# Bucketed attention with a SwiGLU behind it: batch 1's second pair turned and hashed in other slots, one scaling on ScalarE, one pair's loads on ScalarE's queue

## The chip, the core and the metric

The kernel runs on one core of a Trainium2 chip. The core has TensorE (PE, matrix products; PEld is its weight load), VectorE (DVE), ScalarE (ACT), GpSimd (POOL) and SyncE (SP, which here only issues DMAs), each with its own instruction stream that it works through in order. The metric is the device time of one execution in microseconds (us). A comparison of two kernels on this chip tells them apart from about 2%, here 6.8 us.

## The reference

Four batches, eight heads, 768 tokens, head width 64. Each token's query and key is hashed by six sign bits of a projection; a query sees only the keys of its own bucket. The attention output goes through an RMS norm and a SwiGLU with width 1536.

```python
q_bits = (np.einsum('bhsd,dk->bhsk', q, proj) > 0).astype(np.int64)
k_bits = (np.einsum('bhsd,dk->bhsk', k, proj) > 0).astype(np.int64)
q_bucket = np.sum(q_bits * powers, axis=-1)
k_bucket = np.sum(k_bits * powers, axis=-1)
mask = q_bucket[:, :, :, None] == k_bucket[:, :, None, :]
scores = np.where(mask, scale * q @ k.T, -1e9)
attn = softmax(scores)
x = (attn @ v).transpose(0, 2, 1, 3).reshape(B * S, H * D)
xn = x / sqrt(mean(x * x) + 1e-6) * rms_g
g = xn @ w_gate
out = (g * sigmoid(g)) * (xn @ w_val) @ w_out
```

## The kernel before, in words

The mask is folded into the score product: each head's operand (tile QK) has 64 rows of q or k and 12 rows of scaled sign bits, so that a score whose buckets differ is so low that its exponential vanishes. A **pair** (b, hp) is two heads of one batch. For a pair, these steps make QK:

- the raw k and q are loaded (lines 111 and 121, tiles kL and qL);
- they are turned. Batch 0 and the first two pairs of batch 1 are turned by TensorE (`keep_pair`: three transposes at line 169 into a PSUM bank, then a copy by DVE at line 177 into kT or qT); the others by DVE itself from 32-wide blocks (`turn_dve`, line 193, four steps for k and four for q);
- they are cast to 16 bits into QK (lines 183 and 185 in halves by ACT and POOL, or line 201 whole by POOL);
- they are hashed (`hash_pair` or `hash_lone`: eight products at line 209 into d_ps, the signs by DVE at line 216, and eight small SP DMAs, line 267 or 284, that put the bit rows into QK).

A **window** w is half of a batch's queries (w = 2b or 2b + 1). The work runs in 192 **slots**, one for each (window, head, third of the keys): in a slot PE computes the scores of the next slot (line 343, two PSUM buffers), ACT takes their exponential (line 353) and later PE multiplies with v (line 365). The first 48 slots are windows 0 and 1 (batch 0); slots 48 to 71 are window 2. When a pair of heads of a window is done, `attn_out` divides (lines 380 to 401) and `sumsq` sums the squares (line 405). After a window, `norm` takes the sums (DVE, line 412) and the root (POOL, lines 414 and 418), `scale_x` scales three chunks of 128 rows (line 423), `turn_x` turns them (PE line 430, DVE line 431). The SwiGLU of window w starts in slot 24w + 48: gate (line 445, tanh by ACT at line 447), value (line 455, DVE lines 457 and 458), projection (line 469).

The order is written by hand: `at(s, f, ...)` puts a step into slot s, and inside a slot steps go by rank, then by order of entry. Steps with rank under 3 come ahead of the slot's exponential, the others behind it. Since each engine is in order, a step that waits holds up all that was put behind it on its engine. SP's stream holds the k, q and v loads and the bit rows; POOL's holds the casts, half of `attn_out`, the sums of v and the loads of the SwiGLU weights (lines 520 and 526, software DMAs); ACT's holds no DMA between the first microsecond and the last.

PSUM banks for all but scores and attention outputs come from one ring of three ("g"). Raw tiles come from a ring of ten.

Of the kernel before, what the change touches and what calls it, by code (L numbers as in the profile page):

```python
# [43 lines left out]
def kernel(  # L44
# [12 lines left out]
    nc = tc.nc  # L57
# [38 lines left out]
    raw = {}  # L96

    def raw_tile(b, hp, which):
        shape = [128, 24, 32] if which != "v" and (b, hp) not in BY_PE else [128, 2, 6, D]
        raw[b, hp, which] = lpool.tile(shape, FP32, name=which + "L", tag="L")  # L100
        return raw[b, hp, which]
# [10 lines left out]
        else:  # L112
            eng.dma_start(out=t[:, heads[0]], in_=src[:, heads[0]])

    def load_blocks(eng, b, hp, which):
        lt = raw_tile(b, hp, which)
        for hh in range(2):
            src = {"q": q, "k": k}[which][b, 2 * hp + hh].rearrange("(t k) d -> t k d", k=24)
            for dc in range(2):
                p0 = 64 * hh + 32 * dc  # L120
                eng.dma_start(out=lt[p0 : p0 + 32], in_=src[:, :, 32 * dc : 32 * dc + 32])

# [206 lines left out]
    x, ssp, xn, xnT, ht = {}, {}, {}, {}, {}  # L331
# [76 lines left out]
    rstds = {}  # L408
# [11 lines left out]
    def scale_x(w, c):  # L420
        if w not in xn:
            xn[w] = npool.tile([128, 3, DMODEL], FP16, name="xn")
        nc.vector.tensor_scalar_mul(xn[w][:, c, :], x[w][:, c, :], rstds[w][:, c : c + 1])  # L423

    def turn_x(w, c):
        if w not in xnT:
# [146 lines left out]
    def at(s, f, *a, rank=3):  # L573
        plan[s].append((rank, len(plan[s]), lambda: f(*a)))
# [36 lines left out]
    for i, (t, src) in enumerate(((wg, moe_w_gate), (wv, moe_w_val))):  # L611
        at(2 + 4 * i, load_w, t, src, 0, 768)
        at(12 + 9 * i, load_w, t, src, 768, 1536)
        at(33 + 6 * i, load_wo, 6 * i, 6 * i + 6)

    for hp, loads, turns, sv in ((0, (9, 11, 15), (24, 26, 28, 30), 42),
                                 (1, (13, 17, 28), (33, 35, 37, 39), 45)):
        for which, s in zip("kqv", loads):  # L620
            at(s, load_rows, nc.sync, 1, hp, which)
        for i, s in enumerate(turns):
            at(s, keep_pair, 1, hp, i)
            at(s + 1, casts, 1, hp, i)
        at(turns[3] + 2, hash_pair, 1, hp)
        at(sv, v_prep, 1, hp)
        at(sv + 2, v_sum, 1, hp)

    def in_row(loads, s, hash_slot=None):
        return loads, range(s, s + 8), (s + 4, s + 8, s + 9), hash_slot

    work = {
        (1, 2): ((21, 23, 30), (36, 37, 40, 40, 48, 49, 50, 51), (42, 52, 46), 53),
        (1, 3): in_row((42, 44, 47), 52, 61),
        (2, 0): in_row((51, 56, 59), 61), (2, 1): in_row((64, 67, 70), 71, 80),
        (2, 2): in_row((73, 76, 79), 81), (2, 3): in_row((82, 85, 88), 91, 100),
        (3, 0): in_row((94, 98, 102), 106), (3, 1): in_row((104, 108, 112), 116, 125),
# [1 line left out]
    }  # L641
    for (b, hp), (loads, turns, cast_slots, sh) in work.items():
        for which, s in zip("kqv", loads):
            at(s, load_rows if which == "v" else load_blocks, nc.sync, b, hp, which)
        for i, s in enumerate(turns):
            at(s, turn_dve, b, hp, "kq"[i // 4], i % 4, rank=5)
        for which, s in zip("kq", cast_slots):
            at(s, cast_pool, b, hp, which)
        if sh:
            if b == 1:  # L650
                at(sh, hash_lone, b, hp)
            else:
                at(sh, hash_pairs, b, (hp - 1, hp))
        at(cast_slots[2], v_prep, b, hp)
        at(cast_slots[2], v_sum, b, hp)
        if hp % 2:
            at(66 if b == 1 else 48 * b + (17 if hp == 3 else -4), v_mean, b, hp - 1, 4)
# [17 lines left out]
    for w in range(8):  # L675
        for h in range(H):
            end = LAST[w, h] + 3
            at(end - 1, av, w, h, 0, 9)
            at(end, av, w, h, 9, 18)
            if h % 2:  # L680
                at(end, o_step, w, h // 2, rank=4.5)
                if (w, h) != (0, 7):
                    at(end + 6, s_step, w, h // 2, rank=5)
        at(end + (1 if w == 0 else 9), norm, w, rank=5)
        for c in range(3):
            at(end + (3 if w == 0 else 14 + c), scale_x, w, c, rank=5)
            at(end + (7 + c if w == 0 else 17 + 2 * c), turn_x, w, c, rank=1)
        s0 = 24 * w + 48
        seen = set()
        for ft in range(NF):  # L690
            for f, s in ((g_step, s0 + 16 * ft // NF), (v_step, s0 + (32 * ft + 16) // (2 * NF))):
                at(s, f, w, ft, rank=4 if s in seen else 2)
                seen.add(s)
        for i in range(9 if w < 7 else 6):
            c, j = divmod(i, 3)
            at(s0 + 16 + i, project, w, c, 4 * j, 4 * j + 4, rank=1 if i == 8 else 3)
# [61 lines left out]
```

## Time and profile before

| what | value |
|---|---|
| runs | 340.42 us median of three, 337.58 to 343.3 |
| the profiled execution: its time, its span | 339.3 us, 337.5 us |
| granted TensorE clock | 0.999 |
| busy share: PE, DVE, ACT, POOL | 97%, 70%, 62%, 46% |
| exponentials on ACT (line 353) | 192 of 808 ns |
| DMA issues by SP of 32-wide k and q blocks | 80 |
| DMA issues by ACT | 2, both at the ends |

The span is the time from the first to the last instruction of the core; what lies around it is 1.8 us. A row of a timeline gives the start, the length, the engine, the line and operation, the tiles and the count; a bracket at its end gives how long the engine stood idle before it and for whom. A name with q (SPq, POOLq) is a sequencer: it issues or waits and counts as idle. In a row of waits stand the total, the number of times and the longest.

### The profile page before, as it was taken

Reading aid. Unit: us, or ns where it says so; the run is one execution under the profiler, and the core shown is the slowest. Engines: PE = TensorE matmul, PEld = TensorE weight load, DVE = VectorE, ACT = ScalarE, POOL = GpSimd, SP = SyncE. Lnnn points to the kernel's source line nnn. Section 1 sums busy time; section 2 is a strip of 40 time slices with the busy share of each in tenths; the row PEclk is TensorE's granted clock in tenths of the full one; section 3 lists DMA queues with packets and bytes.
Section 4 is the critical chain, followed back from the end, with each engine's and each line's share of the span. In section 5 each row is a group of like instructions: output and inputs, shape, how many; then the busy total and the mean of one; then the engine's idle time right before and its main releaser. Section 6 shows DMA issues by size and latency. Waiting matters only on the chain.

```text
span 337.5 us, 7796 instructions
## 1 busy us (share of the span) xinstructions
PE 326.8 (97%) x2993; PEld 201.0 (60%) x2993; DVE 236.4 (70%) x526; ACT 210.0 (62%) x328; POOL 155.3 (46%) x230
## 2 busy tenths in 40 slices
PE   8999989889999999999999999999999999999995
PEld 7566656455566565566555666566556665655653
DVE  4769798688758896668768897557546663883860
ACT  3789987656666575757666676567667675332321
POOL 4878789836465576245736475613111311110000
PEclk9999999999999999999999999999999999999999
DMA  7999999464376064508243261100010001001002
GB/s 238 330 223 260 169 169 187 75 124 100 79 186 118 15 111 119 104 20 168 69 105 84 44 116 64 35 16 0 33 62 2 3 0 64 33 0 64 32 0 93
DMA packets 80244, 31.36 MB, mean 93 GB/s; under 512 B 65240, under 2 KB 77264, under 8 KB 80208
## 3 DMA queue, kind: packets, MB, share of 16 engines
q1 hardware_dynamic: 76272, 26.09, 31.7%
q0 software_dynamic: 3712, 4.72, 8.8%
q8 instruction: 23, 0.38, 0.5%
q14 instruction: 13, 0.11, 0.1%
q10 hardware_dynamic: 224, 0.07, 0.1%
HBM read 28.32 MB, written 6.29 MB: 103 GB/s over the span
## 4 chain that ended last, share of the span: by engine, by line
PE 85%; DVE 6%; SPq 3%; DMA 2%; ACT 2%; issue 1%; DVEq 0%; ACTq 0%
PE y_ps L469 18%; PE v_ps L455 17%; PE s_ps L343 15%; PE g_ps L445 12%; PE o_ps L365 9%; PE s_ps L445 5%; PE d_ps L209 4%; SPq L267 2%; PE t_ps L169 1%; PE x_ps L430 1%; PE z_ps L336 1%; DMA kL<-in_k_dram 1%; DVE otmp L380 1%; DVE xn L423 1%; ACT psb L353 1%
## 5 line engine op out<-in xcount | busy, mean ns | idle before, releaser
L353 ACT ACTIVATE psb<-s_ps 128x768 f16<-128x768 f32 x192 | 150.8, 808 | 28.1 <-PE s_ps L343 26.9
L343 PE MATMUL s_ps<-QK 76*128 76x384 f16 x384 | 93.5, 325 | 1.3 <-ACT psb L353 0.5
L455 PE MATMUL v_ps<-xnT,wv 128*128 128x384 f16 x384 | 78.1, 326 | 0.1
L469 PE MATMUL y_ps<-wo,ht 128*128 128x512 f16 x276 | 69.2, 379 | 0.3 <-ACT ysb L476 0.3
L389 POOL TENSOR_TENSOR x<-otmp,rcp 128x384 f32<-128x384 f32 x31 | 25.7, 830 | 93.0 <-DVE rcp L385 92.7
L365 PEld LDWEIGHTS <-psb 128*128 128x128 f16 x1152 | 51.6, 97 | 25.5 <-issue 7.5
L447 ACT ACTIVATE t<-g_ps 128x384 f32<-128x384 f32 x72 | 35.3, 490 | 43.6 <-PE g_ps L445 43.4
L458 DVE SCALAR_TENSOR_TENSOR ht<-a,v_ps 128x384 f16<-128x384 f32 x96 | 53.2, 554 | 10.7 <-PE v_ps L455 1.5
L457 DVE SCALAR_TENSOR_TENSOR a<-t,g_ps 128x384 f32<-128x384 f32 x72 | 39.5, 548 | 28.5 <-ACT t L447 28.3
L445 PE MATMUL g_ps<-xnT,wg 128*128 128x384 f16 x288 | 58.6, 325 | 0.7 <-DVE a L457 0.5
L365 PE MATMUL o_ps<-vl,psb 128*128 128x65 f16 x1152 | 56.8, 194 | 0.6 <-DVE otmp L380 0.5
L455 PEld LDWEIGHTS <-wv 128*128 128x128 f16 x384 | 36.4, 97 | 23.9 <-issue 0.5
L445 PEld LDWEIGHTS <-wg 128*128 128x128 f16 x384 | 36.0, 97 | 24.4 <-issue 1.1
L343 PEld LDWEIGHTS <-QK 76*128 76x128 f16 x384 | 31.6, 98 | 16.1 <-issue 3.7
L469 PEld LDWEIGHTS <-ht 128*128 128x128 f16 x276 | 25.9, 97 | 24.0 <-issue 0.6
L476 ACT COPY ysb<-y_ps 128x512 f32<-128x512 f32 x23 | 13.5, 585 | 25.5 <-PE y_ps L469 22.8
L431 DVE TENSOR_TENSOR xnT<-x_ps,gcol 128x512 f16<-128x512 f16 x24 | 16.3, 685 | 15.1 <-PE x_ps L430 15.1
L401 POOL TENSOR_TENSOR sq<-x 128x384 f32<-128x384 f32 x31 | 25.6, 826 | 2.4
L380 DVE TENSOR_TENSOR otmp<-o_ps,cvb 128x390 f32<-128x390 f32 x32 | 17.8, 558 | 8.8 <-PE o_ps L365 8.7
L447 ACT ACTIVATE t<-s_ps 128x384 f32<-128x384 f32 x24 | 11.8, 491 | 18.4 <-PE s_ps L445 17.6
L201 POOL CAST QK<-kT 64x768 f16<-64x768 f32 x20 | 16.8, 838 | 12.4 <-DVE kT L193 6.5
L193 DVE STREAM_TRANSPOSE kT<-kL 128x192 f32<-128x192 f32 x40 | 19.8, 517 | 2.7 <-DMA kL<-in_k_dram 2.7
(80 smaller groups left out, 325.7 us busy)
## 6 DMA issues: line engine op xcount, KB each, us to landing
vL<-in_v_dram SPq DMA_DIRECT2D x16, 384.0 KB
out_dram<-ysb SPq DMA_DIRECT2D x23, 256.0 KB
kL<-in_k_dram SPq DMA_DIRECT2D x40, 96.0 KB
qL<-in_q_dram SPq DMA_DIRECT2D x40, 96.0 KB
kL<-in_k_dram SPq DMA_DIRECT2D x5, 384.0 KB
qL<-in_q_dram SPq DMA_DIRECT2D x5, 384.0 KB
wg<-in_moe_w_gate_dram POOLq DMA_DIRECT2D x2, 768.0 KB, 7.2
wv<-in_moe_w_val_dram POOLq DMA_DIRECT2D x2, 768.0 KB, 8.5
```

Of the source, the lines that this page charges most:

```text
L343: nc.tensor.matmul(ps[:, j, 0:HALF], k_cols(w // 2, h, 2 * p + j), q_cols(w, h), start=True, stop=True,)
L353: nc.scalar.activation(psb[w, h][:, p], sps.pop(g)[:, :, 0:HALF], AF.Exp, scale=ESCALE,)
L365: nc.tensor.matmul(o[:, c, hh, 0:65], psb[w, h][:, jt // 2, jt % 2, 128 * c : 128 * c + 128], vls[b % 2][:, h, v_chunk(b, h, jt), 0:65], s ...
L380: nc.vector.tensor_add(tmp[:, :, :, 0:65], o[:, :, :, 0:65], cvb[b % 2][:, 2 * hp : 2 * hp + 2, 0:65].unsqueeze(1).to_broadcast([128, 3, 2 ...
L389: eng.tensor_mul(xd.rearrange("p c (h d) -> p c h d", h=2), tmp[:, :, :, 0:64], r.to_broadcast([128, 3, 2, 64]),)
L401: nc.gpsimd.tensor_mul(sq, xd, xd)
L445: nc.tensor.matmul(g, wg[:, kt, fs], xnT[w][:, kt], start=(kt == 0), stop=(kt == 3))
L447: nc.scalar.activation(t, g, AF.Tanh, scale=0.5)
L455: nc.tensor.matmul(vv, wv[:, kt, fs], xnT[w][:, kt], start=(kt == 0), stop=(kt == 3))
L457: nc.vector.scalar_tensor_tensor(out=a, in0=t, scalar=1.0, in1=g, op0=ALU.add, op1=ALU.mult)
L458: nc.vector.scalar_tensor_tensor(out=ht[w][:, ft], in0=a, scalar=0.5, in1=vv, op0=ALU.mult, op1=ALU.mult)
L469: nc.tensor.matmul(y, ht[w][:, ft, c * 128 : (c + 1) * 128], wo[:, ft, :], start=(ft == 0), stop=(ft == NF - 1),)
```

## The change

Slots move for batch 1's first three pairs; two steps change their engine.

- Pair (1, 1): the four `keep_pair` go from slots 33, 35, 37, 39 to 31, 32, 33, 34, each with its casts one slot later; its hash goes from 41 to 40. The norm of window 0 stays in slot 39.
- Pair (1, 0): hash stays in slot 32; `v_prep` goes from 42 to 36. Pair (1, 1): `v_prep` goes from 45 to 48 and `v_sum` from 47 to 50.
- Pair (1, 2): q's load goes from slot 23 to 33, v's from 30 to 38; the third DVE turn of k goes from 40 to 37; k's cast goes from 42 to 46; `v_prep` and `v_sum` go from 46 to 52.
- Pair (1, 3): the k and q blocks are issued by ACT instead of SP, one block a slot: k in slots 46 to 49, q in 50 to 53 (before: all four of k in slot 42, all four of q in 44), last in their slot.
- The two halves of w_out are issued by POOL in slots 38 and 49 (before 33 and 39).
- The sum of squares of window 0's third pair comes one slot sooner (37).
- Chunk 1 of window 0 is scaled by ACT (`nc.scalar.mul`, slot 41), the other chunks still by DVE.

```diff
-    def load_blocks(eng, b, hp, which):
-        lt = raw_tile(b, hp, which)
-        for hh in range(2):
+    def load_blocks(eng, b, hp, which, parts=range(4)):
+        lt = raw.get((b, hp, which)) or raw_tile(b, hp, which)
+        for i in parts:
+            hh, dc = divmod(i, 2)
             src = {"q": q, "k": k}[which][b, 2 * hp + hh].rearrange("(t k) d -> t k d", k=24)
-            for dc in range(2):
-                p0 = 64 * hh + 32 * dc
-                eng.dma_start(out=lt[p0 : p0 + 32], in_=src[:, :, 32 * dc : 32 * dc + 32])
+            eng.dma_start(out=lt[32 * i : 32 * i + 32], in_=src[:, :, 32 * dc : 32 * dc + 32])
...
-        nc.vector.tensor_scalar_mul(xn[w][:, c, :], x[w][:, c, :], rstds[w][:, c : c + 1])
+        if (w, c) == (0, 1):
+            nc.scalar.mul(xn[w][:, c, :], x[w][:, c, :], rstds[w][:, c : c + 1])
+        else:
+            nc.vector.tensor_scalar_mul(
+                xn[w][:, c, :], x[w][:, c, :], rstds[w][:, c : c + 1]
+            )
...
-        at(33 + 6 * i, load_wo, 6 * i, 6 * i + 6)
+        at(38 + 11 * i, load_wo, 6 * i, 6 * i + 6)
...
-    for hp, loads, turns, sv in ((0, (9, 11, 15), (24, 26, 28, 30), 42),
-                                 (1, (13, 17, 28), (33, 35, 37, 39), 45)):
+    for hp, loads, turns, sv, ss, sh in (
+        (0, (9, 11, 15), (24, 26, 28, 30), 36, 44, 32),
+        (1, (13, 17, 28), (31, 32, 33, 34), 48, 50, 40),
+    ):
...
-        at(turns[3] + 2, hash_pair, 1, hp)
+        at(sh, hash_pair, 1, hp)
         at(sv, v_prep, 1, hp)
-        at(sv + 2, v_sum, 1, hp)
+        at(ss, v_sum, 1, hp)
...
-        (1, 2): ((21, 23, 30), (36, 37, 40, 40, 48, 49, 50, 51), (42, 52, 46), 53),
-        (1, 3): in_row((42, 44, 47), 52, 61),
+        (1, 2): ((21, 33, 38), (36, 37, 37, 40, 48, 49, 50, 51), (46, 52, 52), 53),
+        (1, 3): in_row((46, 50, 47), 52, 61),
...
-            at(s, load_rows if which == "v" else load_blocks, nc.sync, b, hp, which)
+            if which == "v":
+                at(s, load_rows, nc.sync, b, hp, which)
+            elif (b, hp) == (1, 3):
+                for i in range(4):
+                    at(s + i, load_blocks, nc.scalar, b, hp, which, [i], rank=6)
+            else:
+                at(s, load_blocks, nc.sync, b, hp, which)
...
-                    at(end + 6, s_step, w, h // 2, rank=5)
+                    at(end + (5 if (w, h) == (0, 5) else 6), s_step, w, h // 2, rank=5)
```

## The prediction

> **What bounds the kernel now.** First the busy shares of the page, then a table of stretches (columns: stretch, length, busy us with instructions of PE, PEld, DVE, ACT and POOL, then clock, DMA share, GB/s).
>
> ```profile
> PE 326.8 (97%) x2993; PEld 201.0 (60%) x2993; DVE 236.4 (70%) x526; ACT 210.0 (62%) x328; POOL 155.3 (46%) x230
> ```
>
> ```profile
> 30.00:41.00 11.00, 10.46 (x139) 6.77 (x133) 8.32 (x18) 10.45 (x16) 9.66 (x16) 1.00 1.03 223
> 41.00:54.00 13.00, 11.60 (x140) 7.65 (x137) 12.27 (x29) 10.88 (x17) 10.34 (x16) 1.00 1.03 187
> 54.00:66.00 12.00, 11.70 (x119) 7.16 (x119) 8.67 (x19) 8.07 (x13) 11.29 (x17) 1.00 0.59 98
> 66.00:70.50 4.50, 2.34 (x15) 1.18 (x13) 3.12 (x8) 1.36 (x3) 0.88 (x2) 1.00 0.94 184
> 70.50:100.00 29.50, 29.43 (x275) 17.60 (x274) 21.81 (x51) 18.94 (x30) 17.92 (x24) 1.00 0.53 112
> ```
>
> PE is the bound: 97% over the span, and from 70.5 us on it hardly pauses (29.43 of 29.50). Every moved step lies before that point. From 30 to 41 ACT is full (10.45 of 11.00), from 41 to 54 DVE is (12.27 of 13.00), from 66 to 70.5 nobody is. PE's pauses are 1.40 us in 41 to 54, 0.30 in 54 to 66 and 2.16 in 66 to 70.5: 3.86 us, 1.1% of the time, is about all that can be won back.
>
> The view of waits from 30 to 75 us names what ended the pauses (total, times, longest):
>
> ```profile
> DVE kT L193 <- DMA kL<-in_k_dram: 2.7, 1, 2.7
> ...
> PE m_ps L324 <- DVE bits L216: 1.6, 1, 1.6
> ...
> PE d_ps L209 <- DVE qT L177: 0.9, 1, 0.9
> ```
>
> The timeline gives their places. Round the hash of pair (1, 1) in slot 41, first DVE alone, then all engines, then the scalings and the first gate:
>
> ```profile
> 48.77 0.54 DVE L177 COPY qT<-t_ps 128x384 f32<-128x384 f32 x1
> 49.23 0.15 DVE L412 TENSOR_REDUCE ss<-ssp 128x3 f32<-128x12 f32 x1
> 49.30 0.86 DVE L193 STREAM_TRANSPOSE kT<-kL 128x192 f32<-128x192 f32 x2
> 50.23 0.68 DVE L216 TENSOR_SCALAR bits<-d_ps,thr,scl 128x384 f16<-128x384 f32 x1
> ```
>
> ```profile
> 49.36 0.83 PE L209 MATMUL d_ps<-qT,pq 128*32 128x384 f32 x2 [0.90 <-DVE qT L177]
> 49.56 0.19 POOL L414 TENSOR_SCALAR ms<-ss 128x3 f32<-128x3 f32 x1 [0.99 <-DVE ss L412]
> 49.76 0.80 ACT L353 ACTIVATE psb<-s_ps 128x768 f16<-128x768 f32 x1
> 49.84 0.89 POOL L418 TENSOR_TENSOR rstd<-ms,mhalf 128x3 f32<-128x3 f32 x1
> ```
>
> ```profile
> 50.83 2.67 DVE L423 TENSOR_SCALAR xn<-x,rstd 128x512 f16<-128x512 f32 x3
> ```
>
> ```profile
> 56.03 0.81 PE L445 MATMUL g_ps<-xnT,wg 128*128 128x384 f16 x4 [0.18 <-DVE xnT L431]
> ```
>
> The last products of the hash wait 0.90 us for a copy that stands in DVE's stream behind window 0's last sums. Then come the sums' end (49.23 + 0.15 = 49.38), the root on POOL (to 50.73), the signs and three scalings on DVE (to 53.50), the turns and the first gate at 56.03. The largest pause, with one row of the chain of waits (63.86) for the load:
>
> ```profile
> 54.42 6.86 SPq L267 DMA_DIRECT2D QK<-bits  x9
> 61.39 3.06 SPq L121 DMA_DIRECT2D kL<-in_k_dram  x4
> ```
>
> ```profile
> 63.86 3.29 DMA kL<-in_k_dram
> ```
>
> ```profile
> 67.28 0.52 DVE L193 STREAM_TRANSPOSE kT<-kL 128x192 f32<-128x192 f32 x1 [2.73 <-DMA kL<-in_k_dram]
> 67.64 0.60 DVE L216 TENSOR_SCALAR bits<-d_ps,thr,scl 128x384 f16<-128x384 f32 x1
> ...
> 68.30 0.29 PE L324 MATMUL m_ps<-vsum,ones 128*128 128x260 f16 x1 [1.65 <-DVE bits L216]
> ```
>
> SP is busy with bit rows to 61.28, so pair (1, 3)'s k is issued from 61.39 to 64.45, and its last block lands at 67.15. DVE stands 2.73 us in the first turn (slot 52); the signs of pair (1, 2) behind it give back the PSUM bank that PE wants for m_ps.
>
> **The change part by part.** *The hash's wait.* The four turns of pair (1, 1) come sooner by two to five slots, so the 0.90 us goes. The copies stay on DVE ahead of the sums in both kernels; one DVE turn more comes ahead of them (49.30: two of 0.43), and DVE has 13.00 - 12.27 = 0.73 us of slack to take it. So I leave the sums at 49.2 and the root at 50.7, within half a microsecond. POOL does not delay the root either: one w_out issue stands ahead of it in both kernels, casts and `v_prep` change places, and POOL idled 0.99 us before it (49.56). A turn by TensorE costs:
>
> ```profile
> L169 PE MATMUL t_ps<-ident,kL 128*128 128x128 f32 x36 | 6.3, 286 | 0.0
> ```
>
> The earlier transposes fall where ACT, not PE, is full (30 to 41) and cost nothing while that cover holds; else four sets of three at 6.3 / 12 = 0.53 us each, with as much saved later, so at most a delay within the stretch. The w_out halves are wanted in slot 64 at the earliest; I cost their move at nothing by itself, and in the first rival by what it meets.
>
> What is late next is the scaling that now stands on ACT in slot 41. It waits for the same root, and behind it on ACT stand all further exponentials. The exponential before it ended at 50.56 in this trace; without the hash's wait that is 49.66, and 50.7 - 49.66 = 1.0 us of ACT then passes in the wait. So the 0.90 is spent again: part's net 0, between -0.9 (PE has other work) and +0.7 (the scaling itself comes on top).
>
> *The scaling.* No row has ACT doing it; the nearest two bound it:
>
> ```profile
> L423 DVE TENSOR_SCALAR xn<-x,rstd x24: 399/482/1046, 50.8 to 304.0; 128x512 f16<-128x512 f32 x24
> ```
>
> ```profile
> L476 ACT COPY ysb<-y_ps 128x512 f32<-128x512 f32 x23 | 13.5, 585 | 25.5 <-PE y_ps L469 22.8
> ```
>
> I take 0.59 us on ACT from the row of the same size. On DVE the three took 2.67, so one is worth 0.89, and the signs' 0.68 now comes while POOL takes the root: up to 1.57 us off the path from root to first gate. PE's scores and the exponentials pace the turns in slots 45 to 47, so I count half: -0.8 (0 to -1.6). Page "ScalarE: Activation LUTs", section "Rules for kernel authors", in the Trainium skill says that multiplications belong on VectorE, which is faster per element; the rows above contradict it for this place, since ACT's 585 ns stands against 890 here and 482 in DVE's median. By the rule the part would be worth nothing, and the sum would be 0.8 higher.
>
> *The loads of pair (1, 3).* From SP's queue go eight issues, and ACT gets them, one a slot. k's last block is issued behind the exponential that slot 49 emits:
>
> ```profile
> 58.90 0.81 ACT L353 ACTIVATE psb<-s_ps 128x768 f16<-128x768 f32 x1
> ```
>
> With the 0.8 us from above that is 58.1 + 0.8 = 58.9; 3.29 later, at 62.2, k has landed. DVE came to the turn in slot 52 at 67.28 - 2.73 = 64.55, so 63.75 with the gain: 1.5 us to spare. The wait goes, and with it PE's pause of 2.16: -2.2 (0 to -2.2). Late next would be q's last block, issued in slot 53, turned from slot 56.
>
> The issues cost ACT something:
>
> ```profile
> L121 SPq DMA_DIRECT2D kL<-in_k_dram x40: 571/644/2697, 34.6 to 192.9; - x40
> ```
>
> ```profile
> 53.80:65.80 12.00, 11.66 (x121) 7.09 (x119) 8.84 (x20) 8.27 (x14) 11.29 (x17) 1.00 0.59 100
> ```
>
> Eight at the median 0.644 are 5.15 us. ACT has 12.00 - 8.27 = 3.73 idle in about those slots. If issue and execution never overlap, 1.4 us remain; if the sequencer issues while the last exponential still runs, none. I take +0.5.
>
> **Sum:** 0 - 0.8 - 2.2 + 0.5 = -2.5. The profiled execution took 339.3 us (span 337.5 and 1.8 around it): 336.8. The median of the runs, 340.42, lies 1.1 higher, which gives 337.9. I predict 337.4, between the two: 2.5 under 339.9, the middle of the two times.
>
> **The rivals.** *ACT is blocked by its own issues (slower).* A weight load was under way when SP issued pair (1, 2)'s k. First the durations of these four issues (least, median, greatest ns), then the queues from 36 to 39 us (packets, MB, share of the 16 engines; q0 POOL's, q1 SP's):
>
> ```profile
> L121 SPq DMA_DIRECT2D kL<-in_k_dram x4: 693/1604/2697, 34.6 to 38.7; - x4
> ```
>
> ```profile
> q0 software_dynamic: 312, 0.48, 99.5%
> q1 hardware_dynamic: 2, 0.00, 0.3%
> ```
>
> The issues grew to 2.70 us, and q1 hardly moved. The change puts the second half of w_out in slot 49, just ahead of ACT's four q issues. If these four take 1.6 and the others 0.644, that is 9.0 us against 3.73 idle: +5.3 in place of +0.5, and the sum becomes +2.3, 342.2 from that middle. With all eight slow it is 12.8 - 3.7 = 9.1, 346. It decides once the exponentials are held up by more than 3.0 us in slots 46 to 53. For it: the two loads meet. Against it: one issue a slot leaves ACT's queue time to drain, and issue may overlap with execution. Chance 0.27.
>
> "DMA: Bandwidth & Descriptors" in the Trainium skill, section "Queues, rings and completion order", says that each DMA engine takes packets from its queues in turn; then the weight load would leave the q blocks a share, and this rival would vanish. The trace disagrees, with 99.5% against 0.3%. The same page, section "Issuing engines are not separate DMA queues", says that another issuer saves only time in the issuing sequencer; here that is what is late.
>
> *A wait for landings.* One of SP's issues shows a wait that its data does not need:
>
> ```profile
> SPq L267 <- DMA vL<-in_v_dram: 2.3, 1, 2.3
> ```
>
> Bit rows do not depend on v; it is the eighth issue after that load. If an issue waits for the landing of the one eight before, ACT's first k block may wait for SP's bit rows, which queue behind q's and v's loads that the change put later, and hold the exponentials. With one such wait of 2.3 us beside the forecast: 339.9 - 2.5 + 2.3 = 339.7. For it: eight bit rows of 6.86 / 9 = 0.76 us stand on SP in the slots before. Against: SP starts (1, 0)'s rows sooner, since q and v of (1, 2) no longer stand ahead. Chance 0.15.
>
> *The change doesn't reach what it aims at.* q of pair (1, 2), now loaded ten slots later behind eight bit rows, or k of pair (1, 3) behind the w_out load is late again, DVE waits as before, and 2.2 comes back: 339.6. Chance 0.13.
>
> **How the numbers follow.** Forecast 0.45 at 337.4; blocked ACT 0.27 at 342.2, waits for landings 0.15 at 339.7, missed aim 0.13 at 339.6. All bounds at their best are -0.9 - 1.6 - 2.2 = -4.7: 335.2 from the middle. From there to 343.5, past the four slow issues, only the worst of the first rival and the runs' own scatter (337.58 to 343.3) are left out: 334.5 to 343.5. A measurement tells about 2% from no change, 6.8 us here. Faster by that needs more than all pauses: 0.04. Slower needs all eight issues slow and a further wait: 0.07. Within: 0.89.
>
> **What would show it.** In the changed profile, right: no wait of d_ps for qT near 48 us; ACT waits for POOL's root before a 128x512 operation of 0.6 to 0.7 us; DVE's wait for kL gone or under 0.5; eight ACT issues of about 0.65 with exponentials no more than 1 us late behind them; the first gate near 55. Wrong: issues on ACT over 1.3 us or with pauses ahead of them; a wait of DVE for qL near slot 48 or 56; PE idle between 50 and 70 us above 2 us; the root later than 51.5.

## The result, and the profile after

The kernel after takes 342.0 us (median of six runs, 340.93 to 344.44), the kernel before beside it 338.1: the ratio is 1.0127, with a 95% interval of 1.0089 to 1.0164. By the 2% bound that is no difference; by the interval it is a loss of 3.0 to 5.5 us. The forecast was 337.4, a gain of 2.5. The profiled execution of after took 341.2 us (span 339.4) at a mean granted clock of 1.000. In every comparison, runs over 1.5% above the fastest of their kernel are left out (one of them took 677.6 us).

In the kernel after all line numbers behind line 115 are shifted: the hash products stand in line 208, signs in 215, DVE's turns in 192, scores in 342, exponentials in 352, the two scalings in 423 (ACT) and 425 (DVE), gate, tanh and value in 449, 451 and 459, the block loads in 120. The stretches first, with the columns of the prediction's table:

```profile
41.00:54.00 13.00, 11.05 (x141) 7.33 (x138) 11.03 (x29) 11.23 (x17) 9.84 (x17) 1.00 0.65 109
54.00:66.00 12.00, 9.60 (x99) 6.12 (x98) 7.25 (x16) 6.10 (x10) 8.41 (x11) 1.00 1.21 183
66.00:70.50 4.50, 3.02 (x29) 1.41 (x28) 2.75 (x7) 2.42 (x5) 3.87 (x5) 1.00 1.42 193
70.50:100.00 29.50, 29.34 (x267) 17.39 (x265) 22.16 (x51) 18.68 (x29) 17.81 (x25) 1.00 0.53 99
```

Against the prediction's table, PE from 41 to 54 us does 0.55 us less work than before, from 54 to 66 us 2.10 less, from 66 to 70.5 us 0.68 more. The loss lies in the middle stretch, where PE had been 97% busy; there ACT too falls from 8.07 to 6.10 and idles half the time. The timeline of ACT in that stretch (ACTq is its sequencer issuing a DMA):

```profile
57.49 0.58 ACTq L120 DMA_DIRECT2D kL<-in_k_dram  x1
58.11 0.49 ACT L451 ACTIVATE t<-g_ps 128x384 f32<-128x384 f32 x1 [2.21 <-PE s_ps L342]
...
61.02 0.57 ACTq L120 DMA_DIRECT2D kL<-in_k_dram  x1
61.64 0.49 ACT L451 ACTIVATE t<-g_ps 128x384 f32<-128x384 f32 x1 [2.33 <-PE g_ps L449]
...
66.81 0.57 ACTq L120 DMA_DIRECT2D qL<-in_q_dram  x1
67.48 0.49 ACT L451 ACTIVATE t<-g_ps 128x384 f32<-128x384 f32 x1 [2.35 <-PE g_ps L449]
```

Three times ACT stands for 2.21 to 2.35 us, and each pause ends with one of its own DMA issues, directly ahead of the tanh. The brackets name products of PE, which is no more than the last event on record: the gate products that these three tanhs read had ended at 56.79, 58.42 and 65.24. So in the first pause 0.9 us pass before ACT could have gone on, in the others hardly anything does. About 0.6 us of each is the issue itself; all eight issues took 0.57 to 0.67 us. What each waits for is in the instruction records of the trace: in this program SP's and ACT's DMAs use eight completion semaphores in turn, and an issue waits until the earlier DMA on its semaphore has landed. The issue at 57.49 waits on the semaphore of pair (1, 2)'s third q block, issued by SP at 49.73; those at 61.02 and 66.81 wait on those of bit rows that SP issued at 57.70 and 61.09. The last parts of these three landed at 57.47, 61.00 and 66.79, each 0.02 us ahead of the issue that waited. SP's own timeline shows why they are late, first in the kernel before, then in after:

```profile
41.45 2.66 SPq L121 DMA_DIRECT2D qL<-in_q_dram  x4
```

```profile
48.36 6.13 SPq L120 DMA_DIRECT2D qL<-in_q_dram  x4
54.59 1.32 SPq L111 DMA_DIRECT2D vL<-in_v_dram  x1
56.01 6.57 SPq L266 DMA_DIRECT2D QK<-bits  x8
```

The four q blocks take 6.13 us to issue where the kernel before took 2.66: the change issues them at 48.36, right behind the first half of w_out (48.00 to its landing at 55.84). Pair (1, 1)'s rows start after them.

The other signs: the hash's wait for qT is gone, the root ends at 50.71 (forecast 50.7), and the scaling runs on ACT right behind it, in 0.72 us:

```profile
49.82 0.89 POOL L417 TENSOR_TENSOR rstd<-ms,mhalf 128x3 f32<-128x3 f32 x1
...
50.74 0.72 ACT L423 ACTIVATE xn<-x,rstd 128x512 f16<-128x512 f32 x1
50.74 1.83 DVE L425 TENSOR_SCALAR xn<-x,rstd 128x512 f16<-128x512 f32 x2 [0.19 <-POOL rstd L417]
```

DVE's wait for kL is gone as well. ACT's exponential of slot 48 comes at 55.09, 0.04 us earlier than in the profile of before, that of slot 53 at 67.87, 4.84 later. Of this the missing wait for kL gives back 2.9 by slot 56.

### The profile page after: what moved, and what is told of

Read it like the earlier page. It is cut to its first block, busy times and chain, and to the rows that moved or that the text cites. A ratio compares the mean times of both kernels' runs of the same rounds, so it can differ in the third digit from the quotient of the medians.

```text
span 339.4 us, 7797 instructions
## 1 busy us (share of the span) xinstructions
PE 326.6 (96%) x2993; PEld 200.9 (59%) x2993; DVE 235.6 (69%) x525; ACT 210.6 (62%) x329; POOL 155.3 (46%) x230
## 4 chain that ended last, share of the span: by engine, by line
PE 86%; DVE 4%; DMA 4%; ACT 2%; SPq 1%; issue 1%; POOL 1%; ACTq 0%; DVEq 0%
PE y_ps L473 18%; PE v_ps L459 18%; PE s_ps L342 16%; PE g_ps L449 13%; PE o_ps L364 9%; PE s_ps L449 5%; PE d_ps L208 4%; DMA qL<-in_q_dram 2%; DMA QK<-bits 2%; PE x_ps L434 1%; PE t_ps L168 1%; PE z_ps L335 1%; SPq L266 1%; DVE otmp L379 1%; ACT psb L352 1%
## 5 line engine op out<-in xcount | busy, mean ns | idle before, releaser
L200 POOL CAST QK<-qT 64x768 f16<-64x768 f32 x20 | 16.7, 834 | 9.5 <-DVE qT L192 8.9
```

The lines of the kernel that those rows point to most:

```text
L200: nc.gpsimd.tensor_copy(QK[b, hp][0:64, hh, o : o + S], T0[b, hp, which][64 * hh : 64 * hh + 64, :])
```

## The experiments

*Another look at the kernel before.* Its first profile, on which the prediction rests, took 339.3 us; most of its later runs lie at 337.

> The kernel before once more, for a second profile: the one shown took 339.3, the middle of its later runs is 337.4 where the mean granted clock was 0.998 or more and 340.9 where it was 0.995 or less. A profile at 337 should show DVE's wait for kL or another pause before 72 us shorter by about 2 us; one at 341 a stretch at half clock.

Measured 336.85 us, span 335.0. The timeline of SP and then two stretches:

```profile
43.36 1.10 SPq L111 DMA_DIRECT2D vL<-in_v_dram  x2
44.56 12.36 SPq L267 DMA_DIRECT2D QK<-bits  x16
57.02 4.03 SPq L121 DMA_DIRECT2D kL<-in_k_dram  x4
```

```profile
54.00:66.00 12.00, 11.59 (x119) 7.04 (x116) 9.80 (x21) 8.05 (x14) 11.31 (x17) 1.00 0.73 119
66.00:70.50 4.50, 4.33 (x43) 2.73 (x41) 3.71 (x9) 2.53 (x5) 1.36 (x2) 1.00 0.80 161
```

The pause of 2.73 us before the first turn of pair (1, 3) is not there, and PE works 4.33 of 4.50 us where the first profile had 2.34. Here v's second issue came 0.24 us after that of w_out's first half (44.05 and 43.81) and took 0.41; in the first profile it came 0.89 after it (44.98 and 44.09) and took 1.57, and a bit row then waited 2.3 us for v's landing. The sixteen rows took 12.36 us in place of 14.63, and k came 4.37 us sooner. In the largest comparison 26 runs of before count: 17 from 336.46 to 338.51 us, four from 339.04 to 339.93 at a clock of 0.999 or 1.000, and five from 340.28 to 341.37 at a clock of 0.995 or less. The pause on which the prediction put 2.2 of its gain is in one of two profiles, and the other is the one nearer to most runs.

Set against this second profile, after's exponentials are 0.48 us late at slot 48, 5.12 at slot 53, 4.44 at slot 56 and 4.38 at the last slot; the two times differ by 4.35. So nearly the whole loss of after's profile arises in the slots of ACT's issues.

*The four first runs* take the change apart. Edits are of the kernel after where nothing else is said. Three theories stand against each other in what was expected: L, an issue waits for the landing of the DMA eight before it, and the engine stands meanwhile; I, the issues and the transfers themselves cost the time; R, the turns, the hash and the scaling do.

ACT's issues alone, on the kernel before:

```diff
...
-        (1, 3): in_row((42, 44, 47), 52, 61),
+        (1, 3): in_row((46, 50, 47), 52, 61),
...
+            elif (b, hp) == (1, 3):
+                for i in range(4):
+                    at(s + i, load_blocks, nc.scalar, b, hp, which, [i], rank=6)
```

> The kernel before, with one part alone: the eight blocks of pair (1, 3) issued by ACT in slots 46 to 53; w_out, turns, hash and scaling as in before. L: ACT pauses in front of one to three of its issues, each about as long as SP's bit rows and loads still need to land; DVE's wait for kL (2.7 us in before) goes or shrinks all the same; 339 to 343, slower than before. I: eight issues at 0.6 us against the idle time of ACT, less DVE's wait: 336 to 339. R: as before or better, 336 to 338, no pauses of ACT.

Measured 341.48 against 338.57: ratio 1.0085 [1.0045, 1.0125]. ACT's timeline, a row of PE's waits, and stretches of 2 us:

```profile
53.67 0.63 ACTq L120 DMA_DIRECT2D kL<-in_k_dram  x1
58.70 0.81 ACT L352 ACTIVATE psb<-s_ps 128x768 f16<-128x768 f32 x1 [4.35 <-PE s_ps L342]
```

```profile
PE s_ps L342 <- POOL sq L400: 3.6, 1, 3.6
```

```profile
54.00:56.00 2.00, 0.21 (x7) 0.08 (x3) 1.11 (x2) 0.35 (x1) 1.83 (x3) 1.00 1.24 217
56.00:58.00 2.00, 0.20 (x1) 0.14 (x2) 0.00 (x0) 0.00 (x0) 1.92 (x4) 0.50 0.94 156
```

The time is in the range of theory L: the move of eight issues to ACT costs 2.9 us by itself. Turns, hash, scaling and w_out are as in before, so the explanation by those alone falls. But the long pause of this profile is not the one that L forecast. ACT waits 4.35 us for scores (its next issue comes behind that exponential, at 58.72), and PE waits 3.59 us for bit rows: the instruction records have it wait on the semaphores of three rows of pair (1, 0), which SP issued from 46.99 to 48.71, ahead of the first of ACT's eight issues (53.67), and whose last parts landed at 57.45 to 57.87. Against the second profile of before the exponential of slot 48 is 4.1 us late, and with the lower clock behind the pause the last one is 5.5 late. Whether ACT's issues made those landings later is not shown, and no wait of ACT for a landing holds PE in this profile. The loss of the move is measured, its way in this kernel is open.

SP in the same slots as ACT:

```diff
-                    at(s + i, load_blocks, nc.scalar, b, hp, which, [i], rank=6)
+                    at(s + i, load_blocks, nc.sync, b, hp, which, [i], rank=6)
```

> The kernel after, but the eight blocks of pair (1, 3) are issued by SP, in the same slots 46 to 53. Three theories of why the kernel after takes 342.0 against 338.1. Theory L (landing waits): SP and ACT share eight completion semaphores in turn, so an issue on ACT waits for the landing of the DMA eight before, and ACT's exponentials stand behind it (2.21, 2.33 and 2.35 us in the trace of after). Then here ACT has no idle time that ends with its own issue, the exponentials of slots 49 to 53 come at 57 to 63 as in before (57.27 to 63.03), SP bears the wait instead, k is late by what SP's bit rows take, DVE waits 1 to 3 us for it: 337 to 339. Theory I (the cost of issuing and of the transfers, with any engine): the eight transfers are the same and as late, 340 to 343. Theory R (the earlier turns and the scaling on ACT cost the time): nothing of that is changed, 341 to 343, with PE's pauses before 54 us the same as in before or longer.

Measured 346.46: 1.024 [1.0162, 1.0318], worse than after. ACT no longer stands ahead of an issue, as forecast, but SP comes to these issues only behind its rows, at 62.15, and DVE pays:

```profile
DVE kT L192 <- DMA kL<-in_k_dram: 4.7, 1, 4.7
```

I had written 1 to 3 us for this wait and 337 to 339 for the time. The wait is longer since SP's rows start at 55.81, behind q and v of pair (1, 2), whose issues meet the w_out load. Two stretches at half clock, 3.41 us from 53.18 and 6.83 us from 70.25, are in this time as well.

SP in the slots of before, the rest of the change kept (the ACT branch is taken out as well):

```diff
-        (1, 3): in_row((46, 50, 47), 52, 61),
+        (1, 3): in_row((42, 44, 47), 52, 61),
```

> The kernel after, but the blocks of pair (1, 3) are issued by SP in slots 42 and 44, as in before: what is left of the change is the earlier turns, hash, scaling on ACT and later w_out and q loads. L: no pauses of ACT behind its own issues; k is issued before SP's bit rows of pair (1, 1) or behind them, DVE waits at most 2 us; 336 to 338, no slower than before. I: 337 to 339. R: 341 to 343, since its parts are all still there.

Measured 342.12: 1.0111 [1.0048, 1.0174], a miss: nothing is won back by taking the issues from ACT. The timelines of SP and DVE:

```profile
62.21 3.49 SPq L120 DMA_DIRECT2D kL<-in_k_dram  x4
```

```profile
68.42 0.52 DVE L192 STREAM_TRANSPOSE kT<-kL 128x192 f32<-128x192 f32 x1 [4.10 <-DMA kL<-in_k_dram]
```

The loss stays whole without ACT's pauses, so a second fault stands beside them: k by SP comes 5.2 us later than in the second profile of before (62.21 against 57.02).

w_out back in slots 33 and 39, ACT's issues kept:

```diff
-        at(38 + 11 * i, load_wo, 6 * i, 6 * i + 6)
+        at(33 + 6 * i, load_wo, 6 * i, 6 * i + 6)
```

> The kernel after, with the two w_out loads back in slots 33 and 39, so that the second does not meet the blocks of pair (1, 3). L, where the w_out load is what keeps the landings late: SP's rows and q blocks land sooner, ACT's pauses ahead of its issues shrink from 6.9 us in all to under 3, 338 to 340. L without that (the landings are late because SP's rows are issued late): pauses as in after, 341 to 343. I: the same as after, 341 to 343. R: the same as after.

Measured 340.93: 1.0063 [1.0030, 1.0096], 1.1 us under after (2.2 by the two ratios). Two waits of ACT end with an issue (1.22 and 1.42: 2.6 us in all), where after has five (2.21, 2.33, 0.41, 2.35, 0.60: 7.9). A third wait, 1.64, has an issue in it that ends at 58.54, but the gate products, partly at half clock, end only at 59.06. First these, then one that is the issue's:

```profile
57.96 0.58 ACTq L120 DMA_DIRECT2D kL<-in_k_dram  x1
59.09 0.49 ACT L451 ACTIVATE t<-g_ps 128x384 f32<-128x384 f32 x1 [1.64 <-PE g_ps L449]
...
60.89 0.57 ACTq L120 DMA_DIRECT2D kL<-in_k_dram  x1
61.50 0.49 ACT L451 ACTIVATE t<-g_ps 128x384 f32<-128x384 f32 x1 [1.22 <-PE s_ps L342]
```

The pauses shrink to under 3 us, as forecast for a w_out load that keeps the landings late; the time misses its 338 to 340. In this profile (339.47, the fastest of ten runs) slot 48 is already 2.0 us behind the second profile of before, after a pause of PE of 1.28 us at 50.70 and at half clock from 51.76 to 58.59; ACT's pauses add 0.6. Pair (1, 2)'s last q block still meets a load (2.88 us for that issue alone, at 50.40).

*Is it the landing or the load?* Eight transfers of 16 bytes each, by ACT, on the kernel before:

```diff
+    tiny_t = const.tile([1, 32], FP32, name="tiny")
+    tiny_src = moe_rms_g.rearrange("(o n) -> o n", o=1)
+
+    def tiny(i):
+        nc.scalar.dma_start(
+            out=tiny_t[:, 4 * i : 4 * i + 4], in_=tiny_src[:, 4 * i : 4 * i + 4]
+        )
+
+    for i in range(8):
+        at(46 + i, tiny, i, rank=6)
```

> The kernel before, and eight transfers more that move next to nothing (four floats each, into a tile that nobody reads), issued by ACT in slots 46 to 53. L (an issue waits for the landing of the one eight before, on SP's queue too): ACT pauses one to three times for 1 to 4 us ahead of these issues although they carry 16 bytes, and DVE's wait for kL stays: 341 to 345, PE idle in 54 to 66 us for over 2 us against 0.30. I (the cost lies in issuing and in the blocks' transfers): eight issues of 0.6 us, partly beside ACT's idle time, no pauses: 337.5 to 339.5.

Measured 342.95 against 337.67: 1.0145 [1.0075, 1.0214]. ACT's timeline, and a row of SP's waits from 30 to 80 us:

```profile
57.11 0.81 ACT L353 ACTIVATE psb<-s_ps 128x768 f16<-128x768 f32 x1
59.79 0.22 ACTq L664 DMA_DIRECT2D tiny<-in_moe_rms_g_dram  x1
60.05 0.49 ACT L447 ACTIVATE t<-g_ps 128x384 f32<-128x384 f32 x1 [2.14 <-PE o_ps L365]
```

```profile
SPq L267 <- DMA tiny<-in_moe_rms_g_dram: 4.5, 1, 4.5
```

The tanh's gate products had ended at 58.32, so an issue of 0.22 us that moves 16 bytes holds ACT for 1.7 of the 2.14 us; the row of SP whose semaphore it waits on landed at 59.77. Neither issuing nor the blocks' transfer is the cost. The wait goes both ways: a bit row on SP stands 4.5 us for a 16-byte transfer that ACT had issued (at 53.63, itself late), k is issued at 64.04, and DVE waits 3.3 us for it. Against the second profile of before the exponentials are 1.3 us late at slot 55, 4.3 at slot 56, where k is late, and 6.0 at slot 57, behind a stretch at half clock. So the larger share comes by the lateness of k, on SP's queue, and the clock behind it. The theory that an issue waits for the landing eight before is borne out on both queues.

*Another ring.* POOL's queue uses other semaphores:

```diff
-                    at(s + i, load_blocks, nc.scalar, b, hp, which, [i], rank=6)
+                    at(s + i, load_blocks, nc.gpsimd, b, hp, which, [i], rank=6)
```

> The kernel after, but POOL issues the eight blocks of pair (1, 3), in the same slots 46 to 53. Its queue has other semaphores than SP's and ACT's. L: no pauses of ACT ahead of issues, its exponentials of slots 49 to 53 come as in before (57 to 63 us); the blocks queue behind the second w_out load on POOL's own queue, k lands after 66 and DVE waits for it: 339 to 344 by that wait alone. I: as after.

Measured 343.09: 1.0153 [1.0086, 1.0220]. ACT's timeline and a row of the waits:

```profile
63.55 0.81 ACT L352 ACTIVATE psb<-s_ps 128x768 f16<-128x768 f32 x1
64.65 0.81 ACT L352 ACTIVATE psb<-s_ps 128x768 f16<-128x768 f32 x1 [0.30 <-PE s_ps L342]
71.18 0.49 ACT L451 ACTIVATE t<-g_ps 128x384 f32<-128x384 f32 x1 [5.72 <-PE g_ps L449]
```

```profile
DVE kT L192 <- DMA kL<-in_k_dram: 4.7, 1, 4.7
```

From 52 to 65 us no pause of ACT is longer than 0.95 us, as the landing theory says. Then k is late behind w_out's second half on POOL's own queue (its last block is issued at 59.80, right behind w_out at 58.95), DVE waits 4.7 us, gates and tanh stand behind, and 6.83 us at half clock come with it.

*The hash and the scaling.* Earlier turns and hash, the scaling on ACT, all loads as in before (the ACT branch is taken out as well):

```diff
-        at(38 + 11 * i, load_wo, 6 * i, 6 * i + 6)
+        at(33 + 6 * i, load_wo, 6 * i, 6 * i + 6)
...
-        (1, 2): ((21, 33, 38), (36, 37, 37, 40, 48, 49, 50, 51), (46, 52, 52), 53),
-        (1, 3): in_row((46, 50, 47), 52, 61),
+        (1, 2): ((21, 23, 30), (36, 37, 37, 40, 48, 49, 50, 51), (46, 52, 52), 53),
+        (1, 3): in_row((42, 44, 47), 52, 61),
```

> The kernel before with the earlier turns and hash of pair (1, 1) and the scaling on ACT alone; all loads, w_out's halves and pair (1, 2)'s among them, as in before. The kernel that differs from this one only in w_out and pair (1, 2)'s q and v (and takes pair (1, 3) by SP in the slots of before) took 342.1, with a wait of 4.1 us of DVE for kL. Theory M (the moved loads of w_out and pair (1, 2) are at fault: they push pair (1, 3)'s blocks and the landings back): here the wait for kL is again 2.7 or less, 336 to 338.5. Theory R (turns, hash and scaling are at fault): 340 to 343, with more idle time of PE before 54 us.

Measured 338.82 against 337.67: 1.0028 [0.9993, 1.0063]. No wait of DVE for kL is left in its profile (k is issued at 58.00), which speaks for the moved loads as the second fault. It is not faster either. The timeline round the scaling, and stretches of 2 us:

```profile
51.11 0.72 ACT L423 ACTIVATE xn<-x,rstd 128x512 f16<-128x512 f32 x1 [0.62 <-POOL rstd L417]
...
52.58 0.49 PE L342 MATMUL s_ps<-QK 76*128 76x384 f16 x2 [1.28 <-ACT psb L352]
```

```profile
52.00:54.00 2.00, 1.42 (x15) 0.91 (x15) 1.51 (x4) 1.97 (x3) 1.09 (x3) 0.80 1.25 208
54.00:56.00 2.00, 2.00 (x21) 1.66 (x20) 1.26 (x3) 1.62 (x2) 1.66 (x3) 0.50 1.24 209
56.00:58.00 2.00, 1.82 (x21) 1.10 (x19) 0.99 (x2) 0.81 (x1) 1.88 (x3) 0.85 0.77 134
```

ACT waits 0.62 us for the root and scales for 0.72; the next exponential starts 1.25 us after the end of the one before, PE stands 1.28, and then its granted clock falls to half. All ten runs of this kernel have a mean clock of 0.990 to 0.995. The same with the scaling back on DVE:

```diff
-        if (w, c) == (0, 1):
-            nc.scalar.mul(xn[w][:, c, :], x[w][:, c, :], rstds[w][:, c : c + 1])
-        else:
-            nc.vector.tensor_scalar_mul(
...
+        nc.vector.tensor_scalar_mul(xn[w][:, c, :], x[w][:, c, :], rstds[w][:, c : c + 1])
```

> The earlier turns and hash of pair (1, 1), loads as in before, and all three scalings on DVE. With the scaling on ACT this kernel took 338.8: ACT waited 0.62 us for the root, the scaling took 0.72, PE stood 1.28 us and the granted clock fell to 0.50 between 53 and 57 us. Theory S (the scaling on ACT makes PE stand, and the pause lowers the clock): PE's pause near 51 us is under 0.9, the clock stays at 1.0, 336 to 337.5, no slower than before. Rival: the pause or the lower clock comes from the earlier hash itself: 338 to 339.5, clock again near 0.994.

Measured 337.24 against 338.10: 0.9969 [0.9932, 1.0005]. Its timelines of ACT and DVE, and the stretch from 54 to 66 us:

```profile
49.65 4.36 ACT L352 ACTIVATE psb<-s_ps 128x768 f16<-128x768 f32 x6 [0.72 <-PE s_ps L342]
...
51.08 2.42 DVE L422 TENSOR_SCALAR xn<-x,rstd 128x512 f16<-128x512 f32 x3 [0.19 <-POOL rstd L417]
```

```profile
54.00:66.00 12.00, 11.56 (x120) 7.10 (x120) 9.39 (x21) 7.49 (x13) 9.92 (x13) 1.00 0.72 119
```

Six exponentials in a row, no pause of PE over 0.7 us between 40 and 85, clock 1.00. Between these two kernels only the scaling differs: on ACT it costs 1.6 us by the medians (0.6% by the two ratios, whose intervals overlap by 0.1%), the stretch at half clock included.

*Could it beat both?* The kernel just shown beats after; against before its interval reaches 1.0005, so a gain is likely but not shown. Two more runs tried to keep v's issue out of the w_out load, with the halves in slots 35 and 41:

```diff
-        at(33 + 6 * i, load_wo, 6 * i, 6 * i + 6)
+        at(35 + 6 * i, load_wo, 6 * i, 6 * i + 6)
```

> As the last, with w_out's halves in slots 35 and 41 in place of 33 and 39, so that v of pair (1, 2) is issued before the first half starts. If runs of 339 and more come from v's issue meeting the w_out load (then SP's rows wait 2.3 us and pair (1, 3)'s k is 3 to 4 us later), they become rarer: median 336 to 337.3, highest below 339. Rival: the later second half delays pair (1, 3)'s k instead: 338 to 341, DVE's wait for kL over 2 us.

> The kernel before with w_out's halves in slots 35 and 41, alone. In a second profile of before, at 336.9, v of pair (1, 2) was issued at 43.4 to 44.5 us, just ahead of the w_out load, and no wait for kL was there; in the first, at 339.3, v's second issue at 45.0 took 1.57 and DVE waited 2.7. If that meeting makes the difference, the median falls to 336.5 to 337.3 and no run lies at 339 with a clock of 0.998 or more. Rival: the later second half delays k: 338 to 340.

On top of the kernel with the earlier hash: 337.72, 0.9985 [0.9955, 1.0015]. On the kernel before: 337.29, 0.9997 [0.9959, 1.0034], three of twelve runs at 339.23 or more. Neither is told apart from before. Two of these three runs had a clock of 0.999 or 1.000, against what I expected. That v's meeting with the w_out load makes the slower runs of before is thus seen in two profiles but not shown by a run.

## Why the prediction was wrong, step by step

**What bounds the kernel: the wrong execution.** The table of pauses was read rightly, but it was one execution's. The sum was set against 339.9, between a profile at 339.3 and a median of three runs at 340.42. The median of before was 338.10, 338.57, 337.67 and 338.10 in the four comparisons, and its second profile, at 336.85, has no wait for kL. Some 2 us of the error are there before any step of the change.

**The hash's wait, net 0 (-0.9 to +0.7): the net about right, in part by luck.** The row of d_ps waiting for qT is gone, sums and root come as forecast. But the exponential that was to end at 49.66 ends at 50.62 in after: those of slots 38 to 41 had come 1.2 us later than in before, so the 0.90 was spent ahead of the root, most likely by the earlier turns, and not in ACT's wait for it, which is 0.12. With the scaling on DVE the part measures -1.0 (-2.3 to +0.2), at the lower bound.

**The scaling, -0.8 (0 to -1.6): wrong sign.** The step "so I count half" credited the shorter way from root to first gate. The runs show +1.6, with w_out in its early slots: the exponentials behind the scaling on ACT are what PE waits for at that place, and the clock falls behind the pause. In after's own profile the scaling is cheaper: ACT waits 0.12 for the root, the clock stays at 1.00, and slot 48 is 0.48 late. The working for the part before had counted ACT's wait at 1.0 (0.62 measured) and the scaling on top as the bad bound, +0.7, and then let the other term cancel it. Duration: 0.72 us on ACT, not 0.59. The Trainium skill's rule that a multiplication belongs on VectorE ("ScalarE: Activation LUTs", "Rules for kernel authors"), which the prediction held against its own rows, came out right here, though not by the time of one instruction (0.72 against 0.81 to 0.92 on DVE): by what stands behind it.

**The loads off SP, -2.2: the mechanism holds, the gain was not there.** DVE's wait for kL is gone in after, but in the second profile of before it had not been there.

**ACT's issues, +0.5: the step that failed.** It priced the issuing (eight times 0.644 less idle time). The issues took 0.57 to 0.67, as said, and are not the main cost. ACT stands for landings: 2.21, 2.33 and 2.35 us in three places, of which some 1.8 is issuing and 0.9 the gate's, and from slot 48 to 53 its exponentials fall 4.6 us further behind the second profile of before. Alone on the kernel before, the move costs 2.9 us (1.5 to 4.2), though its one profile shows another pause, and 16-byte transfers in its place cost 4.9 (2.5 to 7.2). The second rival named this mechanism, down to the waiting on SP's bit rows, but with one wait of 2.3 and a chance of 0.15; there were eight issues, each with an issue eight before it, and a load under way for most of them. The first rival's time, 342.2, came out, by the wrong way: no issue on ACT was long. Its long issues were SP's: 2.52 and 2.20 us for pair (1, 2)'s third and fourth q block.

**w_out's halves and pair (1, 2)'s loads at nothing: too cheap.** With w_out early, 1.1 us of the loss go (2.2 by the ratios); with SP issuing pair (1, 3) as before, the kernels with and without these moved loads stand at 342.1 and 338.8. The loads meet, SP's stream slips by 4 us (k issued at 62.21 against 58.00), and whatever comes behind on either queue is late. The parts overlap: by the ratios, +0.9 for hash and scaling, +2.9 for ACT's issues and +2.8 for the moved loads (w_out's among them) make 6.6, against 3.0 to 5.5 measured for the whole. That ACT's pauses and k's lateness take each other's place would explain it; no run shows it.

## What to carry to other kernels

Before a DMA is put on an engine that computes, ask what its issue waits for, not how long it takes: here eight semaphores shared by SP and ACT tied ACT's tanh and the exponentials behind it to the landing of another queue's transfer, and issues of 16 bytes cost no less than issues of blocks. Before a pause is counted as a gain, look whether a second execution has it: the largest one of the first profile was absent in the second. Before a pause is put down to the engine that a bracket names, look which semaphore ended it: a wait of PE for 3.59 us was put down to POOL and ended with bit rows that SP had issued some ten us before. And a short operation put into the stream of the engine that paces PE can cost its wait and its length there, however much time it frees elsewhere.

## What the runs showed of the hardware that was not expected

PE's granted clock fell to 0.50 for 3.41 us after a pause of no more than 1.28 us (the kernel with the scaling on ACT, from 53.19 us), and for 6.83 us after a pause of 3.59 (ACT's issues on the kernel before, from 55.99 us). With SP in ACT's slots it fell at 53.18 though no pause there was over 0.78. It did not fall after 1.65 us in the first profile of before, nor after 1.46 and 1.48 in after. Between a kernel's first and last microseconds, every stretch at 0.50 in the profiles lasts 3.41 or 6.83 us. "TensorE: Matmul & The Clock Gate" in the Trainium skill, section "Part 1: The HAM clock gate (the "warmup" mystery)", says that the clock halves after an idle window of about 3.4 us; the pause of 3.59 agrees, those of 1.28 and 0.78 do not. What decides for the shorter pauses is not settled by these runs. Of a kernel's spread a part is this: of the 26 runs of before, the five over 340 us are the five with a mean clock of 0.995 or less.

A transfer of 16 bytes, issued at 53.63 us, had its semaphore waited for until 57.06, 3.4 us, while the w_out load was under way (it landed at 58.05). The bit row that SP issued at 46.99 us in the profile with ACT's issues alone landed at 57.45, all but its last part by 54.49; the wait for it ended with that last part.
